# Scales shared out for several token blocks by one product, at other slots, and a larger ring of pieces for two weights

## The chip, the cores and the metric

One Trainium2 chip, one core of it. The metric is device time in microseconds of one execution, reference inputs, median over the runs shown. TensorE is PE in the profile, VectorE DVE, ScalarE ACT, GpSimd POOL, and SyncE (which issues the transfers) SP.

## The reference

Strided and local attention over 4 sequences of 576 tokens with 8 heads of 64, and behind it two feed-forward layers on the 2304 tokens of width 512. The first has 2048 hidden columns and the second 1536:

```python
h = x @ w_in
x = (h * np.cos(h)) @ w_out
g = x @ w_gate
y = (g * (1.0 / (1.0 + np.exp(-g))) * (x @ w_val)) @ w_out
```

The weights come as 8-byte words. The kernel multiplies in 16-bit floats: every operand is scaled by a power of two, split into a high and a low part, and three matmuls (high by high, high by low, low by high) stand for one product. For each split the kernel needs the largest magnitude of the whole operand on all 128 partitions.

## The kernel before, in words

The tokens lie in five blocks, three of 512 and two of 384 (`BLOCKS`), numbered 0 to 4. After attention comes **layer one**: for each block 16 slots, one for each 128 hidden columns. A slot is an up-projection `up1` (12 matmuls into a PSUM bank), an activation chain on ACT, DVE and POOL (`up1_a` on ACT, `up1_b` on DVE L577, `up1_c` on ACT, `up1_d` on DVE L584, `up1_e` on ACT and POOL L589), and, some slots later, a contraction `down1` (12 matmuls into four accumulators). The number of slots between (`lag`) shrinks from 12 to 2, so some slots hold two contractions. **Layer two** then runs over the same blocks, in six slots each, with products of halves of gate and val weights that a slot loads in one transfer.

PE runs strictly in the order of the code. It has four PSUM banks from `bank()` for the up-projections. A bank is free again when the last reader, L584 of two slots on, is done.

A scale is found in four steps. DVE reduces each 128x512 piece of the operand to one column (`scale_pieces`, L521, for tokens; `scan_raw`, L174, for weights). `spread_tops` (L120 to L130) reduces these columns to one, makes it a power of two and multiplies a 128x128 identity by it. `common_scale` (L136) multiplies the result by a matrix of ones on PE, into a whole PSUM bank, and DVE reduces that bank (L137) and makes the scale from it (L112 to L114). These products stand in PE's order between the contraction of one slot and the up-projection of the next. Token scales are `sx` (input of layer one) and `sy` (input of layer two), one per block.

While PE does layer one, the other engines prepare the weights. Work for that stands in a queue `fill`, with a cost for each step, and `pump` takes as many steps per slot as a share of the slot's matmul time pays for (`SHARE`, `SHARE2`). Token scales and splits stand in a second queue, `urgent`, of which one step is taken per slot (`pump_urgent`). In `fill` come, in this order, the conversion of w_out, the scans of gate and val, their scales, the twelve halves of gate and val (`pairs_later`), the scans of w_out2, its scale, and its conversion (`seven_later`). A half of gate and val goes through ACT (`g0`, L224), DVE (`g2` L231 and `g3` L235), four sums on POOL (L918), ACT (L245) and DVE (L248), and is then stored to DRAM. Its pieces live in a ring of homes, `unit_free`; a home that was stored comes back when the store has landed. Homes below `UNIT` (16) serve the activations, homes 16 to 23 are this ring, eight in all.

Of the kernel before, what the change touches and what calls it, by code (L numbers as in the profile page):

```python
# [59 lines left out]
HOMES, LATE, UNIT = 24, 4, 16  # L60
# [19 lines left out]
def build(tc, qk_l, qk_s, v_l, v_s, w_in, w_out, w_gate, w_val, w_out2, mask_l, mask_s, eye32, eye16, out):  # L80
    nc = tc.nc
    wide = w_in.dtype != F32
    with ExitStack() as ctx:
# [23 lines left out]
        def brief(name):  # L107
            return small.tile([128, 1], F32, name=name, bufs=2)

        def finish_scale(p, bound):  # L110
            s, inv = col("s"), col("inv")
# [5 lines left out]
        def spread_tops(parts, words):  # L117

            m, p = brief("m"), brief("p")
            nc.vector.tensor_reduce(out=m, in_=parts, op=ALU.max, axis=AX.X)  # L120
            if words:
                a = brief("a")
# [6 lines left out]
            d = small.tile([128, 128], BF16, name="tops", bufs=2)  # L129
            nc.vector.tensor_scalar(out=d, in0=id16, scalar1=p, scalar2=None, op0=ALU.mult)  # L130
            return d

        def common_scale(d, bound):

            t, p = bank()[:, 0:128], brief("q")
            nc.tensor.matmul(out=t, lhsT=ones16, rhs=d, start=True, stop=True)  # L136
            nc.vector.tensor_reduce(out=p, in_=t, op=ALU.max, axis=AX.X)  # L137
            return finish_scale(p, bound)
# [9 lines left out]
        parts_w = {k: small.tile([128, a.shape[0] + 1], F32, name=f"pw_{k}") for k, a in MATS.items()}  # L148
# [51 lines left out]
        def conv_steps(mat, j, dst, scan, free=load_raw):  # L200
# [38 lines left out]
            return box, [(0, g0)] + [(0.63, g1)] * scan + [(0.36, g2), (0.63, g3)]  # L239
# [45 lines left out]
        def top_later(mat):  # L285
            begin([])
            later(0.6, lambda: tops.__setitem__(mat, spread_tops(parts_w[mat], wide)))

        def scale_later(mat, bound):
            later(0.6, lambda: scale_w.__setitem__(mat, common_scale(tops[mat], bound)))  # L290
# [3 lines left out]
        def direct_later(mat, j, tiles):  # L294
# [4 lines left out]
            if j == 0:  # L299
                steps.append((0.6, lambda: scale_w.__setitem__(mat, common_scale(tops[mat], TW_OUT))))  # L300
# [214 lines left out]
        def scale_pieces(blk, scales):  # L515
            parts = small.tile([128, KC + 1], F32, name=f"parts{count[0]}_{blk}")
            count[0] += 1
            box = {}
            nc.gpsimd.memset(parts[:, KC:], TINY)
            for k in range(KC):  # L520
                yield 0.65, lambda k=k: nc.vector.tensor_reduce(out=parts[:, k:k + 1], in_=xy[blk][:, k, :], op=ALU.max, axis=AX.X,  # L521
                                                                apply_absolute_value=True)
            yield 0.6, lambda: box.__setitem__("top", spread_tops(parts, False))
            yield 0.6, lambda: scales.__setitem__(blk, common_scale(box["top"], TX))
# [234 lines left out]
        for j in range(M1):  # L759
            chain_later("in", j, wi)  # L760
            for cost, fn in list(scale_pieces(0, sx)) if j == XSAT else list(split_pieces(0, sx, xs)) if j == XSAT + 1 else ():
# [3 lines left out]
        scale_later("in", TW_IN)  # L765
# [95 lines left out]
        unit_free = deque(range(UNIT, HOMES))  # L861
# [76 lines left out]
        def open_weights(lag):  # L938

            if lag + 4 <= UNIT:  # L940
                most[0] = UNIT
            if not opened and most[0] == UNIT and max(taken, default=0) < UNIT:
                opened.append(True)
                scale_later("gate", TW_IN)
                scale_later("val", TW_IN)
# [5 lines left out]
            if len(opened) == 1 and lag < LATE and max(taken, default=0) < LATE:  # L951
# [4 lines left out]
                scale_later("out2", TW_LAST)  # L956
# [35 lines left out]
        def down_next():  # L992
# [18 lines left out]
        for blk in range(NBLK):  # L1011
            for m in range(M1):
# [11 lines left out]
                if m == (2 if blk else XM) and blk + 1 < NBLK:  # L1024
                    urge(scale_pieces(blk + 1, sx))
# [295 lines left out]
```

## Time and profile before

| | |
|---|---|
| median of 3 runs | 900.95 us (889.18 to 901.86) |
| profiled execution | 890.52 us, of which the span is 888.7 us |
| busy, of the span | PE 856.2 us (96%), DVE 657.0 (74%), ACT 521.9 (59%), POOL 197.9 (22%) |
| granted clock, mean | 0.987 |
| chain that ended last | PE 54%, DVE 3%, ACT 1%, POOL 1% |

A share of busy time is a mean over stages. Attention fills the first 110 us, layer one runs to about 506 us, layer two from there. A matmul counts as busy while it streams, so what matters on PE is the idle time before an instruction, what ended it, and the granted clock.

### The profile page before, as it was taken

To read this page: it belongs to the slowest core of one execution; us is meant where nothing else is said; L and a number is where in the kernel's file an instruction comes from. 1 tells how busy PE (TensorE), PEld (TensorE's weight loads), DVE (VectorE), ACT (ScalarE), POOL (GpSimd) and SP (SyncE) were. 2 spreads that over 40 slices of the span, in tenths; PEclk is the share of its full clock that TensorE was granted. 3 is DMA by queue.
4 is the path that set the end of the run, shared out by engine and by line. 5 is a ranking of instruction groups with operands and counts; after the bars stand their busy time and mean duration, and the time that the engine had idled before them with its cause. 6 is when DMAs were issued, how large, how long until landed. Compare 5 with 4: busy or idle time off the path is not lost.

```text
span 888.7 us, 18462 instructions
## 1 busy us (share of the span) xinstructions
PE 856.2 (96%) x7228; PEld 606.1 (68%) x7228; DVE 657.0 (74%) x1287; ACT 521.9 (59%) x1046; POOL 197.9 (22%) x253
## 2 busy tenths in 40 slices
PE   7999999999999989889999998999999999999998
PEld 4766644444444434445656687888888899999998
DVE  4987889994859977986999578757766665665562
ACT  4888988853446667555788566544544434544440
POOL 3443324221236545522222200000000000000000
PEclk7999999999999989999999999999999999999999
DMA  9998842576626555563445745666777678888894
GB/s 302 363 311 247 259 154 72 181 220 239 237 87 218 192 178 176 156 216 128 134 163 201 267 167 215 231 232 235 262 242 261 232 247 286 309 301 306 314 331 155
DMA packets 53512, 200.61 MB, mean 226 GB/s; under 512 B 5456, under 2 KB 16208, under 8 KB 49584
## 3 DMA queue, kind: packets, MB, share of 16 engines
q1 hardware_dynamic: 53424, 199.42, 65.9%
q8 instruction: 57, 0.93, 0.4%
q14 instruction: 31, 0.25, 0.1%
HBM read 175.41 MB, written 23.99 MB: 224 GB/s over the span
## 4 chain that ended last, share of the span: by engine, by line
PE 54%; DVE 3%; issue 1%; ACT 1%; POOL 1%; ACTq 0%; POOLq 0%; DVEq 0%
PE acc L694 14%; PE bank L541 10%; PE bank L543 10%; PE bank L542 10%; PE acc L541 4%; PE acc L543 4%; PE acc L542 4%; DVE arena L667 1%; DVE arena L1189 0%; POOL arena L918 0%; DVE arena L248 0%; DVE xs L248 0%; DVE wi L611 0%; ACT arena L664 0%; ACT arena L245 0%
## 5 line engine op out<-in xcount | busy, mean ns | idle before, releaser
L541 PE MATMUL bank<-xs,wi 128*128 128x256 f16 (+3 forms) x780 | 234.1, 300 | 16.5 <-DVE q L137 10.1
L543 PE MATMUL bank<-xs,wi 128*128 128x256 f16 (+3 forms) x780 | 234.3, 300 | 0.0
L542 PE MATMUL bank<-xs,wi 128*128 128x256 f16 (+3 forms) x780 | 234.2, 300 | 0.0
L589 POOL TENSOR_TENSOR arena<-tb,arena 128x512 f16<-128x512 f32 (+1 forms) x80 | 91.5, 1144 | 250.9 <-ACT arena L588 235.6
L542 PEld LDWEIGHTS <-wi 128*128 128x128 f16 x880 | 86.3, 98 | 55.8 <-issue 23.0
L541 PE MATMUL acc<-arena 128*128 128x512 f16 (+1 forms) x320 | 115.0, 359 | 0.0
L542 PE MATMUL acc<-arena 128*128 128x512 f16 (+1 forms) x320 | 114.7, 358 | 0.0
L543 PE MATMUL acc<-arena 128*128 128x512 f16 (+1 forms) x320 | 114.5, 358 | 0.0
L541 PEld LDWEIGHTS <-wi 128*128 128x128 f16 x880 | 86.3, 98 | 36.1 <-issue 1.7
L543 PEld LDWEIGHTS <-wi 128*128 128x128 f16 x880 | 86.4, 98 | 35.8 <-issue 1.6
L694 PEld LDWEIGHTS <-arena 128*128 128x128 f16 x1080 | 100.7, 98 | 8.2
L679 POOL TENSOR_TENSOR wi<-tb 128x256 f32<-128x256 f32 (+1 forms) x30 | 20.2, 674 | 340.6 <-DVE tb L661 340.6
L661 DVE SCALAR_TENSOR_TENSOR tb<-tb,c,arena 128x512 f32<-128x512 f32 (+1 forms) x60 | 41.6, 693 | 62.9 <-ACT tb L656 62.7
L574 ACT ACTIVATE tb<-bank,quarter,c 128x512 int32<-128x512 f32 (+1 forms) x75 | 54.4, 725 | 48.8 <-PE bank L543 37.1
L542 PEld LDWEIGHTS <-arena 128*128 128x128 f16 x600 | 58.8, 98 | 34.4 <-issue 1.9
L694 PE MATMUL acc<-arena 128*128 128x256 f16 (+1 forms) x702 | 82.0, 265 | 0.0
L543 PEld LDWEIGHTS <-arena 128*128 128x128 f16 x600 | 58.8, 98 | 33.1 <-issue 0.5
L541 PEld LDWEIGHTS <-arena 128*128 128x128 f16 x600 | 58.8, 98 | 33.0 <-issue 0.7
L664 ACT ACTIVATE arena<-tb 128x256 f16<-128x256 f32 (+3 forms) x59 | 28.9, 489 | 79.6 <-DVE tb L661 79.6
L1189 DVE TENSOR_TENSOR arena<-bank,cv 128x512 f32<-128x512 f32 (+1 forms) x60 | 38.1, 635 | 44.9 <-PE bank L543 44.3
L588 ACT ACTIVATE arena<-tb 128x512 f16<-128x512 f32 (+1 forms) x80 | 46.6, 582 | 38.3 <-PE acc L543 36.5
L541 PE MATMUL bank<-xs,arena 128*128 128x256 f16 (+1 forms) x240 | 62.9, 262 | 1.2 <-DVE arena L1189 1.2
(147 smaller groups left out, 1713.4 us busy)
## 6 DMA issues: line engine op xcount, KB each, us to landing
wi<-w SPq DMA_DIRECT2D x20, 1792.0 KB
arena<-w SPq DMA_DIRECT2D x60, 576.0 KB, 5.3
raw<-w_out SPq DMA_DIRECT2D x56, 512.0 KB, 4.5
arena<-w SPq DMA_DIRECT2D x10, 1792.0 KB
raw<-w_gate SPq DMA_DIRECT2D x24, 512.0 KB, 4.5
raw<-w_val SPq DMA_DIRECT2D x24, 512.0 KB, 4.8
w<-arena SPq DMA_DIRECT2D x42, 256.0 KB, 3.2
raw<-w_in SPq DMA_DIRECT2D x16, 512.0 KB
```

Source lines behind the costliest of these rows:

```text
L541: nc.tensor.matmul(out=o, lhsT=w[:, 0, c], rhs=x[0], start=first, stop=False, **kw)
L542: nc.tensor.matmul(out=o, lhsT=w[:, 0, c], rhs=x[1], start=False, stop=False, **kw)
L543: nc.tensor.matmul(out=o, lhsT=w[:, 1, c], rhs=x[0], start=False, stop=last, **kw)
L574: nc.scalar.activation(out=c["w"].bitcast(I32), in_=c["ph"], func=AF.Identity, scale=turn[c["blk"]], bias=quarter)
L588: nc.scalar.activation(out=g[:, 0, 0:n], in_=w, func=AF.Copy)
L589: nc.gpsimd.tensor_tensor(out=g[:, 1, 0:n], in0=w, in1=g[:, 0, 0:n], op=ALU.subtract)
L661: nc.vector.scalar_tensor_tensor(out=t, in0=t, scalar=s_g[c["blk"]], in1=c["C"][m][:, 1, 0:c["n"]], op0=ALU.mult, op1=ALU.mult)
L664: nc.scalar.activation(out=to, in_=src, func=AF.Copy, scale=2.0 ** -11)
L667: nc.vector.scalar_tensor_tensor(out=to, in0=hi, scalar=-2048.0, in1=src, op0=ALU.mult, op1=ALU.add)
L679: nc.gpsimd.tensor_tensor(out=t_sums[:, 0, 0:h], in0=c["t"][0][:, h:2 * h], in1=c["t"][0][:, 0:h], op=ALU.subtract)
L694: nc.tensor.matmul(out=o[:, c], lhsT=w[:, 256 * i + 128 * c:256 * i + 128 * c + 128], rhs=unit(u)[:, x:x + h], start=j == c == i == 0, sto ...
L1189: nc.vector.tensor_tensor(out=c["C"][m][:, :, h * right:h * right + h], in0=p, in1=t, op=ALU.add)
```

## The change

- `spread_tops`, `common_scale` and `finish_scale` take `n` operands: n columns, n scaled identities side by side, one product of 128n columns, one reduction to n columns.
- The scales of blocks 2, 3 and 4 for layer one are made together in block 1 (two scans to a slot). Before, block b+1's was made in block b.
- Layer two's scale of block 0 is made from slot 8 of block 3 on; those of blocks 1, 2 and 3 together from slot 4 of block 4 on (`MINLAG + 2`). Before, each followed the last contraction of its block. Block 4's stays in layer two.
- Gate's and val's scales are made by one product, after the scans of both.
- `FREE` = 12 takes the place of `UNIT` = 16 for the ring: homes 12 to 23, twelve in all. The ring opens when the activations need at most 12 homes.
- Costs that pace `fill`: gate's and val's scans 1.3 instead of 1.7; `g2` and `g3` of their conversion 0.5 and 0.8 instead of 0.36 and 0.63.

```diff
-HOMES, LATE, UNIT = 24, 4, 16
+HOMES, LATE, UNIT, FREE = 24, 4, 16, 12
...
-            d = small.tile([128, 128], BF16, name="tops", bufs=2)
-            nc.vector.tensor_scalar(out=d, in0=id16, scalar1=p, scalar2=None, op0=ALU.mult)
+            d = small.tile([128, 128 if n == 1 else 384], BF16, name="tops" if n == 1 else "tops3", bufs=2 if n == 1 else 1)
+            d = d[:, 0:128 * n].rearrange("p (n c) -> p n c", n=n)
+            for i in range(n):
+                nc.vector.tensor_scalar(out=d[:, i], in0=id16, scalar1=p[:, i:i + 1], scalar2=None, op0=ALU.mult)
             return d
 
-        def common_scale(d, bound):
-
-            t, p = bank()[:, 0:128], brief("q")
+        def common_scale(d, bound, n=1):
+
+            t, p = bank()[:, 0:128 * n].rearrange("p (n c) -> p n c", n=n), brief("q", n)
             nc.tensor.matmul(out=t, lhsT=ones16, rhs=d, start=True, stop=True)
             nc.vector.tensor_reduce(out=p, in_=t, op=ALU.max, axis=AX.X)
...
-            return box, [(0, g0)] + [(0.63, g1)] * scan + [(0.36, g2), (0.63, g3)]
+            return box, [(0, g0)] + [(0.63, g1)] * scan + ([(0.5, g2), (0.8, g3)] if mat in ('gate', 'val') else [(0.36, g2), (0.63, g3)])
...
-        unit_free = deque(range(UNIT, HOMES))
+        unit_free = deque(range(FREE, HOMES))
...
-            if lag + 4 <= UNIT:
-                most[0] = UNIT
-            if not opened and most[0] == UNIT and max(taken, default=0) < UNIT:
+            if lag + 4 <= FREE:
+                most[0] = FREE
+            if not opened and most[0] == FREE and max(taken, default=0) < FREE:
                 opened.append(True)
-                scale_later("gate", TW_IN)
-                scale_later("val", TW_IN)
+                scale_later(TW_IN, "gate", "val")
...
-                scan_later(mat, j, 1.7)
-            top_later(mat)
+                scan_later(mat, j, 1.3)
+        top_later("gate", "val")
...
             if m == M1 - 1:
-                if blk < NBLK - 1:
-                    urge(scale_pieces(blk, sy))
-                else:
-                    late_scale.extend(scale_pieces(blk, sy))
+                if blk == NBLK - 1:
+                    late_scale.extend(scale_pieces([blk], sy))
...
                 if m == (2 if blk else XM) and blk + 1 < NBLK:
-                    urge(scale_pieces(blk + 1, sx))
+                    if blk == 0:
+                        urge(scale_pieces([1], sx))
+                    elif blk == 1:
+                        urge(scale_pieces([2, 3, 4], sx, 2))
                     urge(split_pieces(blk + 1, sx, xs), ("xs", blk + 1))
+                if blk == NBLK - 2 and m == M1 // 2:
+                    urge(scale_pieces([0], sy))
+                if blk == NBLK - 1 and m == MINLAG + 2:
+                    urge(scale_pieces([1, 2, 3], sy, 2))
```

What becomes of the order of instructions is seen at three places. Line numbers of the change are its own: there L142 is the product, L143 its reduction, L559 to L561 the matmuls, L595 and L602 the steps `up1_b` and `up1_d`, L240, L244 and L257 the conversion and split of weights.

**Gate's and val's scales, on DVE.** Before (the step `up1_d`, L584, stands ahead of both reductions):

```order
L577 SCALAR_TENSOR_TENSOR tb<-bank,c_2528,tb 128x512
L521 TENSOR_REDUCE parts_0_3090<-xy_66 128x1
L120 TENSOR_REDUCE m<-pw_val 128x1
L130 TENSOR_SCALAR tops<-id_76,p 128x128
L584 SCALAR_TENSOR_TENSOR tb<-tb,bank 128x512
L137 TENSOR_REDUCE q<-bank 128x1
L137 TENSOR_REDUCE q<-bank 128x1
L231 TENSOR_SCALAR arena<-arena 128x512
```

The change:

```order
L595 SCALAR_TENSOR_TENSOR tb<-bank,c_2527,tb 128x512
L136 TENSOR_SCALAR tops_3264<-id_76,p_3259 128x128 x2
L143 TENSOR_REDUCE q_3268<-bank 128x2
L240 TENSOR_SCALAR arena<-arena 128x512
L244 SCALAR_TENSOR_TENSOR arena<-raw,arena 128x512
L602 SCALAR_TENSOR_TENSOR tb<-tb,bank 128x512
L240 TENSOR_SCALAR arena<-arena 128x512
L244 SCALAR_TENSOR_TENSOR arena<-raw,arena 128x512
L257 SCALAR_TENSOR_TENSOR arena<-arena,s_3271 128x512
L240 TENSOR_SCALAR arena<-arena 128x512
L244 SCALAR_TENSOR_TENSOR arena<-raw,arena 128x512
```

One reduction stands where two stood, one slot earlier in the program, and it and the first conversion now stand ahead of `up1_d`; seven more steps of conversion and split follow in the same slot.

**A layer-one scale in the middle of the conversion of gate and val, on PE** (block 3's, `sx`; the same slot in both). Before:

```order
L543 MATMUL acc_3758<-arena 128x512
L136 LDWEIGHTS ones_77
L136 MATMUL bank<-tops,ones_77 128x128
L541 LDWEIGHTS wi
L541 MATMUL bank<-xs,wi 128x512
```

The change:

```order
L561 MATMUL acc_3754<-arena 128x512
L559 LDWEIGHTS wi
L559 MATMUL bank<-xs,wi 128x512
```

The product is gone from there, and so are the other token products between gate's and val's scales and the end of their twelve halves (layer two's of blocks 0 and 1).

**The end of layer one, on DVE.** The change makes three `sy` scales there, in the last eight slots of block 4:

```order
L595 SCALAR_TENSOR_TENSOR tb<-bank,c_4917,tb 128x384
L537 TENSOR_REDUCE parts_5076<-xy_69 128x1 x2
L602 SCALAR_TENSOR_TENSOR tb<-tb,bank 128x384
L595 SCALAR_TENSOR_TENSOR tb<-bank,c_4917,tb 128x384
L124 TENSOR_REDUCE m_5494<-parts_5076 128x3
L132 TENSOR_SCALAR p_5495<-m_5494 128x3
L136 TENSOR_SCALAR tops_5498<-id_76,p_5495 128x128 x3
L602 SCALAR_TENSOR_TENSOR tb<-tb,bank 128x384
L595 SCALAR_TENSOR_TENSOR tb<-bank,c_4917,tb 128x384
L143 TENSOR_REDUCE q_5535<-bank 128x3
```

Before, these slots carried the last of w_out2's conversion, which in the change ends some five slots earlier.

## Rows read from the trace of the kernel before

**Rows 1.** The page: busy time, share of the span, instructions.

```profile
PE 856.2 (96%) x7228; PEld 606.1 (68%) x7228; DVE 657.0 (74%) x1287; ACT 521.9 (59%) x1046; POOL 197.9 (22%) x253
```

**Rows 2.** Stretches: length, busy PE PEld DVE ACT POOL (count), clock, DMA share, GB/s.

```profile
250.00:300.00 50.00, 49.59 (x229) 22.39 (x229) 42.57 (x72) 31.58 (x53) 28.38 (x29) 1.00 0.53 174
300.00:356.00 56.00, 51.46 (x225) 22.64 (x225) 46.72 (x75) 37.93 (x62) 30.92 (x31) 0.94 0.55 183
356.00:386.00 30.00, 24.66 (x121) 12.01 (x118) 24.67 (x42) 17.01 (x30) 13.20 (x16) 0.94 0.53 167
386.00:506.00 120.00, 117.86 (x727) 71.02 (x726) 101.98 (x200) 86.51 (x147) 30.51 (x33) 1.00 0.52 183
506.00:560.00 54.00, 48.60 (x435) 42.21 (x433) 39.73 (x70) 31.03 (x50) 3.64 (x5) 1.00 0.54 202
```

**Rows 3.** PE's waits, 200 to 500 us: total us, times, longest.

```profile
PE bank L541 <- DVE q L137: 10.1, 8, 4.1
PE bank L541 <- DVE tb L584: 2.8, 4, 1.6
PE bank L136 <- DVE tb L584: 0.3, 1, 0.3
```

**Rows 4.** PE in order of time: start, duration, instruction, [idle before it, releaser].

```profile
204.77 0.22 PE L136 MATMUL bank<-tops,ones 128*128 128x128 bf16 x1
205.37 0.38 PE L541 MATMUL bank<-xs,wi 128*128 128x512 f16 x1 [0.38 <-DVE q L137]
205.59 0.38 PE L542 MATMUL bank<-xs,wi 128*128 128x512 f16 x1
...
313.59 0.22 PE L136 MATMUL bank<-tops,ones 128*128 128x128 bf16 x1 [0.26 <-DVE tb L584]
317.87 0.58 PE L541 MATMUL bank<-xs,wi 128*128 128x512 f16 x1 [4.06 <-DVE q L137]
...
381.29 0.32 PE L541 MATMUL bank<-xs,wi 128*128 128x384 f16 x1 [2.78 <-DVE q L137]
...
452.70 0.32 PE L541 MATMUL bank<-xs,wi 128*128 128x384 f16 x1 [1.38 <-DVE q L137]
```

**Rows 5.** Two short stretches with a low clock, columns as in rows 2.

```profile
316.50:324.00 7.50, 6.13 (x16) 2.16 (x16) 5.45 (x13) 3.82 (x6) 2.81 (x4) 0.54 0.54 193
381.30:385.30 4.00, 4.00 (x14) 1.85 (x14) 2.45 (x7) 0.39 (x1) 0.75 (x2) 0.57 0.58 167
```

**Rows 6.** DVE in order of time around two products.

```profile
249.65 0.29 DVE L137 TENSOR_REDUCE q<-bank 128x1 f32<-128x128 f32 x1 [6.58 <-PE bank L136]
...
312.86 0.68 DVE L584 SCALAR_TENSOR_TENSOR tb<-tb,bank 128x512 f32<-128x512 f32 x1
...
317.54 0.28 DVE L137 TENSOR_REDUCE q<-bank 128x1 f32<-128x128 f32 x1
```

**Rows 7.** DVE by line and shape, 250 to 360 us (last: attention): busy, mean ns.

```profile
L248 DVE SCALAR_TENSOR_TENSOR arena<-arena,s 128x512 f16<-128x512 f32 x29 | 24.1, 837 | 5.0 <-ACT arena L245 5.0
L235 DVE SCALAR_TENSOR_TENSOR arena<-raw,arena 128x512 int32<-128x512 int32 x21 | 17.7, 841 | 0.3
L231 DVE TENSOR_SCALAR arena<-arena 128x512 int32<-128x512 int32 x22 | 14.9, 677 | 9.8 <-ACT arena L224 9.8
L521 DVE TENSOR_REDUCE parts<-xy 128x1 f32<-128x512 f32 x4 | 2.7, 672 | 0.0
L521 DVE TENSOR_REDUCE parts<-xy 128x1 f32<-128x384 f32 x4 | 2.2, 539 | 0.0
...
L443 DVE TENSOR_REDUCE mx<-bank 128x3 f32<-128x288 f32 x21 | 9.5, 451 | 8.0 <-PE bank L438 7.8
```

**Rows 8.** Waits of ACT (first row) and DVE, 250 to 380 us.

```profile
ACT arena L224 <- DMA w<-arena: 15.6, 13, 4.6
...
DVE arena L231 <- ACT arena L224: 10.6, 10, 2.9
DVE arena L248 <- ACT arena L245: 6.6, 4, 2.8
```

More of the change, by code (lines that the diff above doesn't have):

```diff
@@ L105, in col, with brief, cols, finish_scale @@
             return small.tile([128, 1], F32, name=f"{name}{count[0]}")
[L107 to L111, printed above, removed]
+        def brief(name, n=1):
+            return small.tile([128, n], F32, name=f"{name}{n}", bufs=2)
+        def cols(name, n):
+            count[0] += 1
+            return small.tile([128, n], F32, name=f"{name}{count[0]}")
+        def finish_scale(p, bound, n=1):
+            s, inv = cols("s", n), cols("inv", n)
             nc.vector.reciprocal(out=s, in_=p)
@@ L147, in build @@
         MATS = {"in": w_in, "out": w_out, "gate": w_gate, "val": w_val, "out2": w_out2}
-        parts_w = {k: small.tile([128, a.shape[0] + 1], F32, name=f"pw_{k}") for k, a in MATS.items()}
+        parts_w = {k: small.tile([128, a.shape[0] + 1], F32, name=f"pw_{k}") for k, a in MATS.items() if k not in ("gate", "val")}
+        parts_two = small.tile([128, 2, M2 + 1], F32, name="pw_two")
+        parts_w.update((k, parts_two[:, i]) for i, k in enumerate(("gate", "val")))
         for k, a in MATS.items():
@@ L299, in direct_later @@
             if j == 0:
-                steps.append((0.6, lambda: scale_w.__setitem__(mat, common_scale(tops[mat], TW_OUT))))
+                steps.append((0.6, lambda: set_scales(TW_OUT, mat)))
             steps.append((0, lambda: hi_part(tiles[j][:, 0], box["c"], scale_w[mat][0])))
@@ L513, in build, with scale_pieces, piece @@
         sx, xs, sy, ys = {}, {}, {}, {}
-        def scale_pieces(blk, scales):
-            parts = small.tile([128, KC + 1], F32, name=f"parts{count[0]}_{blk}")
-            count[0] += 1
+        def scale_pieces(blks, scales, at_once=1):
+            n = len(blks)
+            parts = cols("parts", n * (KC + 1)).rearrange("p (n k) -> p n k", n=n)
             box = {}
[L519 to L524, printed above, removed]
+            nc.gpsimd.memset(parts[:, :, KC:], TINY)
+            todo = [(i, k) for i in range(n) for k in range(KC)]
+            def piece(some):
+                for i, k in some:
+                    nc.vector.tensor_reduce(out=parts[:, i, k:k + 1], in_=xy[blks[i]][:, k, :], op=ALU.max, axis=AX.X,
+                                            apply_absolute_value=True)
+            for i in range(0, len(todo), at_once):
+                yield 0.65 * at_once, lambda some=todo[i:i + at_once]: piece(some)
+            yield 0.6, lambda: box.__setitem__("top", spread_tops(parts if n > 1 else parts[:, 0], False, n))
+            yield 0.6, lambda: scales.update(zip(blks, common_scale(box["top"], TX, n)))
         def split_pieces(blk, scales, dst):
@@ L760, in build @@
             chain_later("in", j, wi)
-            for cost, fn in list(scale_pieces(0, sx)) if j == XSAT else list(split_pieces(0, sx, xs)) if j == XSAT + 1 else ():
+            for cost, fn in list(scale_pieces([0], sx)) if j == XSAT else list(split_pieces(0, sx, xs)) if j == XSAT + 1 else ():
                 later(cost, fn)
```

24 lines of the change are left out of this document (14 added, 10 removed).

## The prediction

> **What bounds the kernel now.** I read the page first, then PE's waits by releaser, then PE in order of time around each wait, and last DVE, ACT and the granted clock around the longest ones. PE is busy for 856 of 888.7 us [rows 1], so there are 32 us to gain on PE without removing a matmul, and the question is which of them the edit touches. Between 200 and 500 us PE waits 13.2 us in all: 10.1 us in eight waits for L137, the reduction behind a spreading product, and 3.1 us for `up1_d` [rows 3]. In the rest of its idle time the edit changes nothing but layer two's first slots.
>
> The order of time shows how a product costs PE anything. The product takes 0.22 us. The next up-projection takes the bank that the product used, so it starts when DVE has reduced it: 0.38 us of idle time where DVE stood ready, as at 205.37 [rows 4]. Where DVE was behind, PE waited for all that stood ahead of L137 in DVE's order: 4.06 us at 317.87, 2.78 at 381.29, 1.38 at 452.70 [rows 4]. At 313.59 the product was already issued while DVE had just ended `up1_d`, and it came to L137 only at 317.54 [rows 6]. Both long waits lie in the conversion of gate and val, and behind both the granted clock is low: 0.54 over 7.5 us, 0.57 over 4 us [rows 5]. The levels are 1.2 and 2.4 GHz, so a mean of 0.54 is the low one for 0.92 of the stretch. Ahead of each drop PE had been idle for some 4 and 3 us; behind a wait of 1.6 us [rows 3] the clock between 356 and 386 fell only in that second place [rows 2, 5].
>
> DVE is why L137 came late. From 250 to 386 us it is busy for 114 of 136 us (42.6 + 46.7 + 24.7) [rows 2], and of its 22 idle us 17.2 are waits for ACT [rows 8], which itself waits 15.6 us in thirteen places for stores to free a home of the ring [rows 8].
>
> **The sum, against the profiled execution (890.5 us).**
>
> *Products that go.* The eight waits are 10.1 us [rows 3]: 8.2 in the three long ones, and five of about 0.38 [rows 4]. All these products leave their place: minus 10.1.
>
> *Products that stand instead.* Four are followed by an up-projection: three blocks together (384 columns), gate with val (256), w_out2 and layer two's block 0 (128 each). More columns cost twice. A matmul of 512 columns takes 0.22 us from start to start [rows 4], so 256 more are 0.11. DVE reduces 128 columns in 0.28 us [rows 6] and 288 in 0.451 [rows 7], some 1.05 ns a column, so 256 more are 0.27. That makes 0.38 + 0.38 = 0.76 for three blocks, 0.38 + 0.05 + 0.13 = 0.57 for the pair, and 0.38 each for the other two: plus 2.1. The lower bound is 0 (the next up-projection finds another bank), the upper one a late DVE for one of them, as at 381.29: plus 2.4 more, with 1.7 for the clock. I take 2.1, because the first two stand where DVE waits for PE (6.58 us ahead of L137 at 249.65 [rows 6]) and the others where it is busy for 102 of 120 us [rows 2]. The three-block product at the end of layer one is followed by contractions, which need no bank: nothing.
>
> *Clock.* Low for 0.92 x 7.5 = 6.9 us and 0.86 x 4 = 3.4 us [rows 5]. In the first, PE was idle for up to 1.4 us anyway (7.5 - 6.13). Half of the rest is lost: about 2.9 + 1.7 = 4.6 (4.4 to 5.1). Without the long waits it comes back: minus 4.6.
>
> *Waits for `up1_d`.* Now 3.1 us [rows 3]. Three things move. (a) Eleven token scans leave the stretch, seven of 512 and four of 384 columns: 7 x 0.672 + 4 x 0.539 = 6.9 us [rows 7]; what is left on DVE is about 107 us. (b) The twelve halves themselves (24 L231, 24 L235, 36 L248 of 512: 16 + 20 + 30 us [rows 7]) now fall on 19 slots instead of 21, because scans no longer use up their credit: two slots of matmuls less to hide under, some 10 of the 121 us that PE works at full clock there (125.7 [rows 2] less 4.6), and two `up1_b` and `up1_d` less on DVE, so about 104 against 111. (c) Twelve homes should take most of ACT's wait for stores, and with it DVE's 10.6 [rows 8]. With a third of the 17.2 left DVE needs 110 of 111 us. It starts late: the joint reduction waits for PE with a conversion behind it, so the slot's seven further steps, some 5 us, run into the next one. The four banks let DVE run late by a slot or so, about 5 us. I therefore leave 3.0 us of such waits in, as now. Bounds: 0, and 3 + two thirds of 17.2 less the spare us = 13, if the larger ring frees nothing.
>
> *Costed at nothing.* Layer two's scans of blocks 0 and 1 come into 386 to 506 us, eight of 0.672, and block 4's four of 0.539 leave: plus 3.2 of 18 idle us of DVE [rows 2]; if that cover were gone, w_out2's conversion, which now ends some five slots sooner, would give the time back. Block 2's split comes later in block 1, but its 13 urgent steps, one a slot from slot 2 on, end at slot 14 of 16. Scans of three blocks add 5 us to DVE in block 1; behind them it waited 6.58 us for PE [rows 6]. Layer two's first slots lose a product and its scans. PE idles 5.4 us there (54 - 48.6 [rows 2]); a gain of 0 to that is possible, and I take 0, since the sums and splits of block 1's tokens, which fill those slots, stay where they are. On SP one load of layer two's weights passes behind one store, and POOL loses two small memsets: nothing.
>
> Sum: -10.1 + 2.1 - 4.6 - 3.1 + 3.0 = -12.7, and 890.5 - 12.7 = **878 us**. The profiled execution lies 10.4 us below the median of the three runs, two of which are near 901 and one at 889; the trace shows nothing of the slower two. Against 900.95, 878 is 2.5% less, against 890.5 it is 1.4%. Within 2% a measurement can't tell it from no change.
>
> **Rivals.**
>
> *The runs' extra 10.4 us stays in the median* (0.27). The trace that I have is of the faster kind. If what makes other runs 901 lies outside 200 to 500 us, the change leaves it: 878 + 10.4 = 888. For it: attention, where transfers and clock could vary, is the same in both. Against it: the waits that go are those behind which the clock fell, so other runs may have lost more there. On this the Trainium skill, "TensorE: Matmul & The Clock Gate", section "What's actually happening", says that the gate's monitor runs free of the kernel's start, so that the same gap can cost differently from run to run; no run here shows it. By that rule the extra could be lost clock behind these waits, and then 878 would hold for every run.
>
> *The lateness was DVE's, not the products'* (0.17). Then the change does not do what it says: L137 only made visible that DVE was behind, and the next up-projections wait for `up1_d` instead. For it: 19 slots instead of 21, and a late start. Against it: 6.9 us of scans gone, and homes. If the two long waits (6.8 us) come back as bank waits, 885; with their 4.6 us of clock, 889.
>
> *Slower than the profiled run: the joint reduction holds DVE* (0.06). In the new order it stands ahead of `up1_d`, the conversion behind it. DVE idles 6.6 us there [rows 6] and the seven steps start after that. If also all 17.2 us of waits for ACT stay [rows 8], DVE needs 104 + 17.2 + 5 = 126 against 111 us, less a slot of slack of 5: 10; with the idle 6.6 not made up, 17, in waits long enough to lose 4.6 us of clock: 878 - 3 + 17 + 4.6 = 897. It decides from 15.6 us of such loss on, since that is what the products give (10.1 + 4.6 + 3.1 - 2.1).
>
> **Numbers.** Forecast 0.45 (874 to 883), extra in the median 0.27 (884 to 892), DVE late 0.17 (884 to 890), slower 0.06 (891 to 905), and 0.05 for more than forecast, below 874, if all small waits and some of layer two's go. The range of 871 to 891 leaves out the slower case and the tails. Faster by over 2%, below 883: the forecast less its upper edge, and the 0.05: 0.47. Slower by over 2%, above 919, needs a second such loss: 0.03. Within: 0.50. The likeliest case alone spans 874 to 883.
>
> **What would show it.** Waits for the reduction of about 2 us in all after 200 us, none above 1; a granted clock of 1.00 from 200 to 500 us; waits for `up1_d` of some 3 us, none above 2; ACT's wait for stores well under 15.6; the gap behind the three-block product near 0.76 us and behind the pair's near 0.57. Wrong would be: a wait of 3 us or more on PE in the conversion of gate and val, whatever it waits for; a clock below 1.00 there; or gaps as forecast and a time that is still near 890, which would put the loss into attention or layer two.

## The result, and the profile after

The changed kernel takes **881.33 us** (median of 4 runs, 880.38 to 883.31). The kernel before, run beside it, takes 898.42 us (889.18 to 901.86). Of undisturbed runs the ratio is **0.9887, with a 95% interval of 0.9838 to 0.9935**: 1.1% faster, against a level of before of 881.33 / 0.9887 = 891.4 us and not against its median here; the first experiment shows why these differ. The forecast of 878 was a gain of 2.5% on the median shown. The time lies in the range of 871 to 891, but the gain is 1.1% and not 2.5%: within the 2% that the prediction named, though its interval lies below 1.

The profiled execution took 880.38 us, 10.1 less than the one of before; 0.7 of this is attention (below). The page, and PE's waits from 200 to 500 us (total us, times, longest), for [rows 1] and [rows 3]; L143, L559 and L602 are the former L137, L541 and L584:

```profile
PE 851.0 (97%) x7223; PEld 604.9 (69%) x7223; DVE 658.8 (75%) x1256; ACT 522.0 (59%) x1046; POOL 202.5 (23%) x249
```

```profile
PE bank L559 <- DVE tb L602: 7.0, 8, 1.7
PE bank L559 <- DVE q L143: 1.5, 3, 0.6
PE acc L559 <- DVE xy L573: 0.7, 1, 0.7
```

The waits for the reduction fell from 10.1 to 1.5 us, and those for `up1_d` rose from 3.1 (2.8 and the product's own 0.3) to 7.0. The stretches that answer to [rows 2], shifted by the time gained (length, then busy time of PE, PEld, DVE, ACT, POOL, and the clock):

```profile
244.00:300.00 56.00, 53.65 (x249) 24.15 (x248) 49.81 (x70) 37.01 (x61) 30.33 (x30) 1.00 0.59 188
300.00:350.00 50.00, 47.74 (x220) 21.37 (x219) 46.95 (x65) 35.59 (x60) 34.54 (x32) 1.00 0.60 209
350.00:386.00 36.00, 33.41 (x181) 17.53 (x180) 31.38 (x56) 20.41 (x36) 11.98 (x12) 1.00 0.67 251
386.00:496.00 110.00, 109.30 (x677) 66.08 (x676) 91.86 (x175) 79.36 (x134) 31.02 (x32) 1.00 0.43 155
496.00:550.00 54.00, 48.59 (x434) 42.20 (x433) 38.18 (x62) 31.14 (x51) 3.64 (x5) 1.00 0.49 181
```

The granted clock is 1.00 in all five, where it was 0.94 in two. DVE is busy for 128 of the first 142 us, so it is still nearly full. Layer two's first slots (the last row) idle 5.4 us on PE, as before.

PE in order of time, for [rows 4]: the four new products' gaps, and between them the longest wait in the conversion of gate and val.

```profile
217.04 0.33 PE L142 MATMUL bank<-tops,ones 128*128 128x384 bf16 x1
218.01 0.38 PE L559 MATMUL bank<-xs,wi 128*128 128x512 f16 x1 [0.65 <-DVE q L143]
...
244.70 0.38 PE L559 MATMUL bank<-xs,wi 128*128 128x512 f16 x1 [0.52 <-DVE q L143]
...
282.59 0.38 PE L559 MATMUL bank<-xs,wi 128*128 128x512 f16 x1 [1.48 <-DVE tb L602]
...
380.99 0.22 PE L142 MATMUL bank<-tops,ones 128*128 128x128 bf16 x1
382.88 0.32 PE L559 MATMUL bank<-xs,wi 128*128 128x384 f16 x1 [1.67 <-DVE tb L602]
...
414.68 0.32 PE L559 MATMUL bank<-xs,wi 128*128 128x384 f16 x1 [0.38 <-DVE q L143]
```

Three blocks cost 0.65, the pair 0.52, layer two's block 0 0.38. The wait of 1.67 follows w_out2's product at 380.99, but it stands under L602 in the table. DVE's order shows why:

```profile
381.75 0.61 DVE L257 SCALAR_TENSOR_TENSOR xs<-xy,s,xs 128x384 f16<-128x384 f32 x1
382.28 0.55 DVE L602 SCALAR_TENSOR_TENSOR tb<-tb,bank 128x384 f32<-128x384 f32 x1
382.75 0.28 DVE L143 TENSOR_REDUCE q<-bank 128x1 f32<-128x128 f32 x1
```

DVE was late, and came to the reduction 1.5 us after the product had ended. PE did not wait for that reduction: it started at 382.88, behind the end of `up1_d` at 382.83 and ahead of the end of L143 at 383.03. So it took another bank than the product's, one that `up1_d` frees. I charge the 1.67 to the product, because the product had taken one of the four banks; that PE would have found one free without it is argued, not shown.

**Where the time came from.** Attention varies from run to run, so I measure from the first matmul behind its end to the end of the span; all that the sum speaks of lies in there. (It belongs to layer one's second slot; the first slot runs some 9 us earlier, inside attention.) That matmul starts here in the kernel before:

```profile
113.67 0.38 PE L541 MATMUL acc<-xs,wi 128*128 128x512 f16 x1 [0.63 <-ACT xy L501]
```

and in the changed one here:

```profile
113.00 0.38 PE L559 MATMUL acc<-xs,wi 128*128 128x512 f16 x1 [0.63 <-ACT xy L514]
```

The rest is then 888.7 - 113.67 = 775.0 us before and 878.6 - 113.00 = 765.6 after: **-9.4 us**. By the terms of the sum: products that went -10.1, new ones +3.2 (0.65 + 0.52 + 1.67 + 0.38), `up1_d` from 3.1 to 5.3 (7.0 less the 1.67): +2.2. That leaves 4.7 for the clock, where the prediction had estimated 4.6; the traces show directly only that it no longer fell. This "rest" is what the experiments below are compared by. It is read from one trace of each kernel; where a kernel was traced twice, the two agree within 0.4 us.

### The profile page after: what moved, and what is told of

Read it like the earlier page. It is cut to its first block, busy times and chain, and to the rows that moved or that the text cites. A ratio compares the mean times of both kernels' runs of the same rounds, so it can differ in the third digit from the quotient of the medians.

```text
span 878.6 us, 18390 instructions
## 1 busy us (share of the span) xinstructions
PE 851.0 (97%) x7223; PEld 604.9 (69%) x7223; DVE 658.8 (75%) x1256; ACT 522.0 (59%) x1046; POOL 202.5 (23%) x249
## 4 chain that ended last, share of the span: by engine, by line
PE 74%; issue 6%; POOL 6%; DVE 5%; DMA 4%; ACT 4%; SPq 0%; POOLq 0%; ACTq 0%; DVEq 0%
PE acc L712 14%; PE bank L559 12%; PE bank L561 11%; PE bank L560 11%; PE acc L559 6%; PE acc L561 6%; PE acc L560 6%; POOL arena L936 3%; PE bank L448 2%; POOL arena L607 2%; PE po L501 2%; DMA vl<-v_l 1%; DMA v_pair<-v_s 1%; DVE arena L257 1%; ACT tb L592 1%
## 5 line engine op out<-in xcount | busy, mean ns | idle before, releaser
L559 PE MATMUL bank<-xs,wi 128*128 128x256 f16 (+3 forms) x780 | 232.6, 298 | 12.2 <-DVE tb L602 7.2
L561 PE MATMUL bank<-xs,wi 128*128 128x256 f16 (+3 forms) x780 | 232.6, 298 | 0.0
L607 POOL TENSOR_TENSOR arena<-tb,arena 128x512 f16<-128x512 f32 (+1 forms) x80 | 94.1, 1176 | 234.0 <-ACT arena L606 213.8
L559 PE MATMUL acc<-arena 128*128 128x512 f16 (+1 forms) x320 | 114.5, 358 | 0.0
L561 PE MATMUL acc<-arena 128*128 128x512 f16 (+1 forms) x320 | 114.5, 358 | 0.0
L559 PEld LDWEIGHTS <-wi 128*128 128x128 f16 x880 | 86.1, 98 | 35.1
L561 PEld LDWEIGHTS <-wi 128*128 128x128 f16 x880 | 86.1, 98 | 34.8
L561 PEld LDWEIGHTS <-arena 128*128 128x128 f16 x600 | 58.7, 98 | 32.8
L559 PEld LDWEIGHTS <-arena 128*128 128x128 f16 x600 | 58.7, 98 | 32.6
L559 PE MATMUL bank<-xs,arena 128*128 128x256 f16 (+1 forms) x240 | 62.9, 262 | 1.2 <-DVE arena L1211 1.2
```

The costliest lines, as they stand in the source:

```text
L559: nc.tensor.matmul(out=o, lhsT=w[:, 0, c], rhs=x[0], start=first, stop=False, **kw)
L561: nc.tensor.matmul(out=o, lhsT=w[:, 1, c], rhs=x[0], start=False, stop=last, **kw)
L607: nc.gpsimd.tensor_tensor(out=g[:, 1, 0:n], in0=w, in1=g[:, 0, 0:n], op=ALU.subtract)
```

## The experiments

The changed kernel differs from the one before in three things that can be set apart: the joint products, the ring of twelve homes instead of eight (the constant `FREE`, 24 - 12), and the costs by which the planner spaces scans (1.3 instead of 1.7) and conversions (0.5 and 0.8 instead of 0.36 and 0.63).

### The kernel before, again

No edit.

> The kernel before, unchanged, in five more rounds, for the spread of its runs. If the spread (889 to 902 us) is lost TensorE clock behind the long waits, the runs' span must fall with their mean granted clock: 12 us more is 24 us more at the low level, so a run of 901 should show a mean clock near 0.96 where 889 shows 0.987. If it comes from the transfers of the attention stage, runs near 901 and near 889 show the same mean clock within 0.005.

891.72 us (12 runs, 888.2 to 898.25) beside 891.1 (29 runs, 886.58 to 900.26); ratio 0.9997 [0.9964, 1.003]. The runs of both with a mean clock of 0.984 or more took 886.6 to 892.3, those with 0.975 or less 896.2 to 900.3. The profiled one is of the second kind, 896.17. PE's waits from 200 to 500 us are what they were, so this run's extra does not lie behind the long waits, as the first theory had it:

```profile
PE bank L541 <- DVE q L137: 10.1, 8, 4.1
PE bank L541 <- DVE tb L584: 2.7, 4, 1.6
PE bank L136 <- DVE tb L584: 0.3, 1, 0.3
```

The clock was lower, as that theory also asked (0.975 against 0.987 over the span), but in attention. Here is its stretch from 12 to 50 us in the trace of before that the prediction was made from:

```profile
12.00:50.00 38.00, 35.15 (x522) 24.87 (x523) 31.06 (x84) 30.56 (x114) 16.52 (x26) 0.87 1.03 357
```

and here in this run:

```profile
12.00:50.00 38.00, 34.62 (x338) 23.65 (x340) 19.63 (x54) 21.26 (x72) 11.49 (x19) 0.55 0.91 310
```

```profile
119.70 0.38 PE L541 MATMUL acc<-xs,wi 128*128 128x512 f16 x1 [0.63 <-ACT xy L501]
```

In these 38 us PE issued 522 matmuls at a clock of 0.87, and 338 at 0.55. The low level lasted about 34 us ((1 - 0.55) x 2 x 38) against 10, and the rest began 6.0 us later; it is 774.7 us long, within 0.4 us of the first trace. The kernel's level is 891: medians of 891.1, 891.51 and 891.55 in three sets of 29, 13 and 11 runs. That the 900.95 was a slow draw of attention's clock follows from this, but no trace of that run was kept.

### The changed kernel, again

No edit.

> The changed kernel once more, in five rounds, for its spread. If what spreads the runs of the kernel before (886.6 to 900.3 us, falling with their mean clock) is the clock in attention, which is the same in both kernels, then the changed kernel spreads as far, 876 to 890 us, also falling with the mean clock, and its median lies 9 to 10 us below the median of before (near 882). If the spread came from the two long waits, its runs stay within 4 us of each other.

884.1 us (6 runs, 880.81 to 895.36) against 891.55 (11 runs); ratio 0.99 [0.9855, 0.9944]. Here too the run with the lowest clock (0.973) is the longest. In the profiled execution, 887.37, the rest began at 119.41 us and not 113.00; it is 765.9 us long, with waits of 7.3 for `up1_d` and 1.5 for reductions. The granted clock was low in two places of attention, 0.78 over 12 to 50 us and 0.74 over 70 to 90, where the first trace of the changed kernel has 0.82 and 1.00. So the spread is there with the change too, 881 to 895 us; the first four runs had little of it. The two theories had asked for 876 to 890, falling with the clock, or for 4 us; the first one holds, some 5 us higher, and the median lies 7.5 us below that of before, where 9 to 10 were expected.

### The products alone

Old costs and the ring of eight homes, joint products as changed:

```diff
-HOMES, LATE, UNIT, FREE = 24, 4, 16, 12
+HOMES, LATE, UNIT, FREE = 24, 4, 16, 16
-            ... + ([(0.5, g2), (0.8, g3)] if mat in ('gate', 'val') else [(0.36, g2), (0.63, g3)])
+            ... + [(0.36, g2), (0.63, g3)]
-                scan_later(mat, j, 1.3)
+                scan_later(mat, j, 1.7)
```

> Only the products are changed (joined, at other slots); ring of eight homes and costs of before. Theory 1: 880 to 884, no wait for a reduction above 1 us, clock 1.00 from 200 to 500 us. Theory 2: DVE as late as before (idle 17 us for ACT in the conversion), and PE's 6.8 us of long waits come back as waits for up1_d, with or without their clock: 885 to 890.

892.16 us (10 runs, 888.46 to 901.51), ratio 1.0001 [0.9962, 1.004]; the rest 774.1 us, 0.9 below the kernel before. The median lies above both theories' ranges, the profiled 888.46 within that of theory 2. PE's waits, 200 to 500 us, and the two longest, in order of time:

```profile
PE bank L559 <- DVE tb L602: 11.0, 7, 3.8
PE bank L559 <- DVE q L143: 1.9, 4, 0.6
```

```profile
315.46 0.38 PE L559 MATMUL bank<-xs,wi 128*128 128x512 f16 x1 [2.26 <-DVE tb L602]
...
370.84 0.32 PE L559 MATMUL bank<-xs,wi 128*128 128x384 f16 x1 [3.79 <-DVE tb L602]
```

The products' waits fell from 10.1 to 1.9, and 11.0 us for `up1_d` stand in their place: the 2.26 close to where the 4.06 of [rows 4] had stood, the 3.79 some 10 us ahead of the 2.78. The clock fell twice again, for some 3.4 us each. By themselves the products' new places were worth 0.9 us: the old ones had mostly made visible that DVE was behind, which is the second rival.

### The ring and the costs without the products

The kernel before, with `FREE = 12`, 1.3, 0.5 and 0.8:

```diff
-HOMES, LATE, UNIT = 24, 4, 16
+HOMES, LATE, UNIT, FREE = 24, 4, 16, 12
-            ... + [(0.36, g2), (0.63, g3)]
+            ... + ([(0.5, g2), (0.8, g3)] if mat in ('gate', 'val') else [(0.36, g2), (0.63, g3)])
-        unit_free = deque(range(UNIT, HOMES))
+        unit_free = deque(range(FREE, HOMES))
-            if lag + 4 <= UNIT:
+            if lag + 4 <= FREE:
...
-                scan_later(mat, j, 1.7)
+                scan_later(mat, j, 1.3)
```

> The kernel before with the ring of twelve homes and the new costs, the products where they were. Theory 1: at least one product in the conversion of gate and val still meets a late DVE: waits for reductions of 6 us or more, clock below 1.00 there, 886 to 891. Theory 2: DVE is in time, waits for reductions fall to about 3 us (eight of 0.38) and the clock stays at 1.00: 879 to 883.

887.77 us (10 runs, 884.79 to 895.66), ratio 0.9949 [0.9917, 0.9982]; the rest 771.6, 3.4 less than before.

```profile
PE bank L541 <- DVE q L137: 9.4, 6, 4.5
PE bank L136 <- DVE q L137: 0.8, 2, 0.4
PE bank L541 <- DVE tb L584: 0.8, 1, 0.8
```

The waits for `up1_d` nearly went, the ones behind products stayed, one of them 4.55 us at 326.90 and one 2.30 at 386.14, with two drops of the clock. That is the first theory. So neither half does it alone: the products alone give 0.9 us and leave the lateness at `up1_d`, the ring and the costs alone give 3.4 and leave it at the products, and both together give 9.4. Beside the ring and the costs the products are worth 6.0 us (771.6 - 765.6).

### The ring alone, at old and at new costs

All as changed but eight homes (`FREE = 16`):

```diff
-HOMES, LATE, UNIT, FREE = 24, 4, 16, 12
+HOMES, LATE, UNIT, FREE = 24, 4, 16, 16
```

> The changed kernel with the ring of pieces back at eight homes (it then opens at 16), costs and products as changed. Theory 1 (the products' places made the gain): no wait for a reduction above 1 us, clock 1.00 from 200 to 500 us, time within 2 us of the changed kernel (880 to 883). Theory 2 (the ring made it: DVE is no longer held by ACT's wait for stores): ACT waits 10 us or more for stores again, waits for up1_d rise from 5.3 by at least 5 us, time 886 to 890.

881.76 us (4 runs, 880.62 to 882.05), ratio 0.987 [0.9816, 0.9924]; the rest 765.5, that of the changed kernel. ACT's wait for the stores that free a home, the 15.6 us of [rows 8], is back in full:

```profile
ACT arena L233 <- DMA w<-arena: 15.6, 9, 3.6
```

In the changed kernel's trace ACT has no such wait over 244 to 380 us. DVE's waits for ACT are 12.7 us with eight homes (7.8 for L240, 4.9 for L257) and 8.1 with twelve (1.9 and 6.2), so the larger ring does give DVE time. But PE's waits are the same without it (6.7 and 1.5). At the new costs the ring costs PE nothing.

The other corner is twelve homes and the joint products at the old costs:

```diff
-            ... + ([(0.5, g2), (0.8, g3)] if mat in ('gate', 'val') else [(0.36, g2), (0.63, g3)])
+            ... + [(0.36, g2), (0.63, g3)]
-                scan_later(mat, j, 1.3)
+                scan_later(mat, j, 1.7)
```

> Products and ring as changed, both costs as before. With the changed costs the ring made no difference (765.5 from the end of attention with eight homes, 765.6 with twelve), and without costs and ring the products gave nothing (774.1). Theory F (at the old costs the steps stand so densely that the ring binds): 769 or less, no drop of the clock between 200 and 500 us. Theory G (the ring is idle in either case and the two costs together make the rest): 772 or more, waits for up1_d of 9 us or more.

885.51 us in one run; the rest 770.2, 4.0 less than with eight homes. PE waits 7.9 us for `up1_d`, its longest 3.80, and the clock falls twice. Neither theory's figures came: the rest lies between them. At the old costs the ring is worth 4 us, at the new ones nothing. In this order the 9.4 us are products 0.9, ring 4.0, costs 4.6; with the costs ahead of the ring they are products 0.9, costs 8.6 and the ring nought.

### The costs one by one

Scans at the old 1.7, so that gate's and val's maxima are spread out as before:

```diff
-                scan_later(mat, j, 1.3)
+                scan_later(mat, j, 1.7)
```

> The changed kernel with one cost put back: gate's and val's scans at 1.7 instead of 1.3. Read by the time from the end of attention to the end of the span, which the clock in attention doesn't touch (before 775.1, changed 765.6, products alone 774.1). Theory A (an earlier start of the conversion is what the costs bring, so that it ends among the 512-token slots): 771 or more. Theory B (fewer conversion steps in each slot are what they bring): 768 or less, waits for up1_d near 5 us.

883.37 us (4 runs, 877.49 to 884.3), ratio 0.9891 [0.983, 0.9952]; the rest is 762.1, 3.5 less than the changed kernel's, and PE waits 2.8 us for `up1_d`, where theory B had asked for 5. That an earlier start of the conversion was the gain (theory A) is refuted at these conversion costs: the old cost of the scans is better. The run times alone don't tell the two apart, 883.37 against 881.33 and 884.1.

The conversion's steps at the old 0.36 and 0.63:

```diff
-            ... + ([(0.5, g2), (0.8, g3)] if mat in ('gate', 'val') else [(0.36, g2), (0.63, g3)])
+            ... + [(0.36, g2), (0.63, g3)]
```

> The changed kernel with the other cost put back: 0.36 and 0.63 for the two conversion steps. From the end of attention: theory A 767 or less; theory B 771 or more, with waits for up1_d of 9 us or more and at least one drop of the clock between 250 and 400 us.

883.35 us (10 runs, 881.1 to 893.9), ratio 0.9918 [0.9879, 0.9956]; the rest 767.3, 1.7 more than the changed kernel's, and 7.6 us of waits in eleven pieces, none above 1.6, with the clock at 1.00. Theory B had asked for 771 or more and a drop of the clock: right in sign, too large, and the figure is nearly theory A's (767 or less). Beside the run with both old costs, 770.2 in the section above, it shows that the two costs don't add. At the old conversion costs the scans at 1.3 gain 2.9 us (770.2 to 767.3), at the new ones they lose 3.5 (762.1 to 765.6); the new conversion costs gain 1.7 us beside scans at 1.3 and 8.1 beside scans at 1.7. So what a cost is worth hangs on where the other one puts the steps.

The same costs moved the other way, so that fewer steps fall into a slot:

```diff
-            ... + ([(0.5, g2), (0.8, g3)] if mat in ('gate', 'val') else [(0.36, g2), (0.63, g3)])
+            ... + ([(0.65, g2), (1.05, g3)] if mat in ('gate', 'val') else [(0.36, g2), (0.63, g3)])
```

> The changed kernel with still higher costs, 0.65 and 1.05: about two slots more for the twelve halves. Theory B: waits for up1_d fall from 5.3 us to 3 or less, 762 to 764 from the end of attention. Theory C (what is left of these waits comes from DVE instructions that GpSimd's stretch, and from the chain through GpSimd, not from the number of steps in a slot): 5 us of waits stay, 765 to 767.

879.67 us (4 runs, 875.75 to 883.26), ratio 0.9863 [0.9799, 0.9926]; the rest 760.1, 5.5 less than the changed kernel's, below the 762 to 764 of theory B, and the lowest of all kernels that compute everything.

```profile
PE acc L559 <- DVE xy L573: 1.6, 1, 1.6
PE bank L559 <- DVE q L143: 1.5, 3, 0.6
PE bank L559 <- DVE tb L602: 1.5, 1, 1.5
```

Of the waits for `up1_d` one of 1.5 us is left. So the changed kernel's 5.3 us came from how many conversion steps the planner put into one slot, with GpSimd's sums in place. Wider spacing also keeps more of the steps apart from the sums: L240 takes 0.645 us on average there and L244 0.848, where they took 0.807 and 0.901. Theory C, by which 5 us would have stayed, is refuted.

### What makes DVE late: GpSimd's sums

The 44 sums of L936 in this stretch run on GpSimd, beside DVE's conversion. Here they write zeros and read nothing:

```diff
-                nc.gpsimd.tensor_tensor(out=out, in0=a, in1=b, op=op)
+                nc.gpsimd.memset(out, 0.0)
```

> The changed kernel with GpSimd's four sums of each half replaced by writes of zeros to the same places: GpSimd reads nothing there, and the products of layer two are not the reference's. If DVE's conversion and split are stretched because GpSimd reads and writes at the same time, their means between 244 and 350 us fall from 0.807, 0.901 and 0.906 us to near the 0.42, 0.68 and 0.74 that they take alone, waits for up1_d fall below 1.5 us and the time from the end of attention to 761 to 763. If only the order and the chain hold DVE, the durations stay above 0.65, 0.85 and 0.85.

881.65 us in one run, with a late attention; the rest 759.6, 6.0 less than the changed kernel's and below the expected 761 to 763. DVE by line and shape over 244 to 350 us (busy, mean ns), in the changed kernel:

```profile
L257 DVE SCALAR_TENSOR_TENSOR arena<-arena,s 128x512 f16<-128x512 f32 x31 | 27.9, 906 | 5.4 <-ACT arena L254 5.4
L244 DVE SCALAR_TENSOR_TENSOR arena<-raw,arena 128x512 int32<-128x512 int32 x22 | 19.8, 901 | 0.3
L240 DVE TENSOR_SCALAR arena<-arena 128x512 int32<-128x512 int32 x23 | 18.6, 807 | 1.9 <-ACT arena L233 1.9
L595 DVE SCALAR_TENSOR_TENSOR tb<-bank,c,tb 128x512 f32<-128x512 f32 x17 | 12.5, 738 | 0.0
L602 DVE SCALAR_TENSOR_TENSOR tb<-tb,bank 128x512 f32<-128x512 f32 x17 | 11.5, 674 | 0.0
```

and without the sums:

```profile
L257 DVE SCALAR_TENSOR_TENSOR arena<-arena,s 128x512 f16<-128x512 f32 x31 | 26.7, 867 | 10.4 <-ACT arena L254 10.4
L244 DVE SCALAR_TENSOR_TENSOR arena<-raw,arena 128x512 int32<-128x512 int32 x22 | 15.1, 687 | 0.3
L595 DVE SCALAR_TENSOR_TENSOR tb<-bank,c,tb 128x512 f32<-128x512 f32 x17 | 12.6, 742 | 0.0
L602 DVE SCALAR_TENSOR_TENSOR tb<-tb,bank 128x512 f32<-128x512 f32 x17 | 11.5, 678 | 0.0
L240 DVE TENSOR_SCALAR arena<-arena 128x512 int32<-128x512 int32 x23 | 10.5, 458 | 3.9 <-ACT arena L233 3.8
```

L244 falls from 901 to 687 ns and L240 from 807 to 458, while L595 and L602, which read one operand from a PSUM bank, stay. So the steps of the conversion are lengthened by what GpSimd does beside them: 4.7 + 8.1 + 1.2 = 14 us over this stretch. Of the waits for `up1_d` in the conversion none is left; the 2.0 us that PE still waits for L602 are 1.67 behind w_out2's product and 0.32 at 447 us.

L257 did not fall to the expected 0.74 us. One GpSimd instruction that reads was kept, the subtraction of `up1_e` (L607), and L257 meets it. Two places of this run, with DVE's and GpSimd's rows put together:

```profile
263.15 1.16 POOL L607 TENSOR_TENSOR arena<-tb,arena 128x512 f16<-128x512 f32 x1 [4.02 <-ACT arena L606]
263.65 1.20 DVE L257 SCALAR_TENSOR_TENSOR arena<-arena,s 128x512 f16<-128x512 f32 x1 [1.01 <-ACT arena L254]
...
268.83 0.74 DVE L257 SCALAR_TENSOR_TENSOR arena<-arena,s 128x512 f16<-128x512 f32 x1
269.20 1.39 POOL L607 TENSOR_TENSOR arena<-tb,arena 128x512 f16<-128x512 f32 x1 [3.61 <-ACT arena L606]
```

The one that begins second is lengthened: L257 takes 1.20 us behind L607 and 0.74 ahead of it, L607 1.39 behind L257 and 1.16 ahead of it. In the changed kernel, the place before the 1.48 us wait of PE at 282.59 shows the sums' part one by one, on DVE:

```profile
277.75 1.32 DVE L257 SCALAR_TENSOR_TENSOR arena<-arena,s 128x512 f16<-128x512 f32 x1 [3.02 <-ACT arena L254]
279.00 0.94 DVE L240 TENSOR_SCALAR arena<-arena 128x512 int32<-128x512 int32 x1
279.98 1.10 DVE L244 SCALAR_TENSOR_TENSOR arena<-raw,arena 128x512 int32<-128x512 int32 x1
281.03 0.92 DVE L240 TENSOR_SCALAR arena<-arena 128x512 int32<-128x512 int32 x1
281.87 0.67 DVE L602 SCALAR_TENSOR_TENSOR tb<-tb,bank 128x512 f32<-128x512 f32 x1
```

and on GpSimd:

```profile
277.80 3.86 POOL L936 TENSOR_TENSOR arena<-arena 128x256 f32<-128x256 f32 x4
```

While the four sums run, every step beside them is long, and `up1_d` stands behind. The experiment also frees ACT of its waits for the sums (10.1 us before, 0.6 here), so its 6 us are not DVE's durations alone; that the durations fall is read directly.

### Holding the joint reduction back, and a better pace

An empty step of cost 2.0 ahead of the pair's product, so that fewer conversion steps share its slot:

```diff
                 opened.append(True)
+                later(2.0, lambda: None)
                 scale_later(TW_IN, "gate", "val")
```

> The changed kernel with an empty step of cost 2.0 ahead of gate's and val's product, so that its reduction and the first conversion stand behind up1_d in DVE's order and fewer steps follow in that slot. If the joint reduction holds DVE (the third rival of the prediction), waits for up1_d fall from 5.3 us by 2 or more and the time from the end of attention from 765.6 to 763.5 or less. If not, it stays within 1 us.

879.54 us in one run; the rest 763.8, 1.9 less than the changed kernel's. The waits early in the conversion went; one of 3.03 us is there at 361.53, with one drop of the clock. Without the 1.20 behind w_out2's product the waits for `up1_d` are 3.3 us, 2.0 less, as expected; the rest misses the expected 763.5 by 0.3. That the joint reduction's hold was what cost this is not shown, because the empty step also moves all the steps behind it. Against it: in the changed kernel the first wait for `up1_d` comes some 37 us after that reduction, and DVE stood idle for 3.02 us just ahead of it (277.75 above), so it was not behind any more. Both remedies together, the empty step and costs of 0.6 and 0.95:

```diff
-            ... + ([(0.5, g2), (0.8, g3)] if mat in ('gate', 'val') else [(0.36, g2), (0.63, g3)])
+            ... + ([(0.6, g2), (0.95, g3)] if mat in ('gate', 'val') else [(0.36, g2), (0.63, g3)])
+                later(2.0, lambda: None)
```

> Candidate: the changed kernel with conversion costs 0.6 and 0.95 and the empty step of 2.0. Waits for up1_d 2 us or less, 760 to 762 from the end of attention (765.6 changed, 760.1 with costs 0.65 and 1.05 alone), median 4 to 5 us below the changed kernel's in the same rounds.

878.65 us (6 runs, 877.02 to 890.29), ratio to the kernel before 0.9855 [0.9804, 0.9905]; the rest 763.1. In the same rounds the changed kernel stood at 884.1 and 0.99 [0.9855, 0.9944]: the intervals overlap, and by the rest the two are 2.8 us apart. PE waits 3.6 us for `up1_d`, where 2 or less was expected, and the rest misses the expected 760 to 762. By the same measure the costs of 0.65 and 1.05 alone, 760.1, are the better version.

## Why the prediction was right or wrong

**The comparison failed first.** The sum started from the profiled 890.5 and gave -1.4%; -1.1% was measured. The forecast of -2.5% came from setting 878 against 900.95, the median of three runs, with the words that the trace shows nothing of the slower two. So the 10.4 us between them were taken as gained, with no row for it. What the runs showed in its place: the kernel's level is 891, its runs get longer as their mean clock falls, and the slow one that was traced lost its time in attention. The first rival had it right in kind: the extra lies in attention, and the edit leaves it. Its number, 888, did not follow, because the extra falls on runs of both kernels by chance; it is not a constant to be added. The prediction weighed lost clock behind the waits that go. The repeated run of before has the same waits and the same rest within 0.4 us, so there the two runs lost the same; all its extra is in attention. The rule of the Trainium skill that was weighed with it ("TensorE: Matmul & The Clock Gate", "What's actually happening"), that the gate's monitor runs free of the kernel's start, may bear on attention; no run here shows whether it does.

**The products' waits** (-10.1) went as forecast, and the drops of the clock with them; the granted clock is 1.00 over 200 to 500 us, and the other terms leave 4.7 us for it (forecast 4.6).

**The new products** (+2.1) cost 3.2. Three blocks 0.65 (forecast 0.76), the pair 0.52 (0.57), layer two's 0.38 (0.38). Behind w_out2's product PE waited 1.67 where 0.38 stood, for a bank that `up1_d` frees; the upper bound had allowed for one late DVE, and this was it, without a loss of clock.

**The waits for `up1_d`** (3.0 left in) came to 5.3, and this is the term of the sum that was mis-sized most. The prediction priced DVE's conversion steps at the means of [rows 7]: 0.677, 0.841 and 0.837. After the change they took 0.807, 0.901 and 0.906; on the 76 steps of 512 columns that is 3.0 + 1.3 + 2.1 = 6.4 us more of DVE. More of them ran beside a GpSimd instruction: 52 of those 76, where it was 41 of the 72 of [rows 7]. That these 6.4 us made the extra 2.3 us of waits is argued, not shown; without the sums the waits go, but with wider spacing and the sums in place they nearly go too. That ACT's wait for stores would go, and DVE would gain by it, came true (DVE's waits for ACT fell from 17.2 to 8.1 us, a third of 17.2 was forecast), but PE gained nothing by it: with eight homes its waits are the same.

**The reason was wrong where the size came out.** Waits for L137 were read as the products' price, and five of 0.38 us were. The two long ones, 6.8 us and their clock, were DVE's lateness, as the second rival had it: the products alone gave 0.9 us. But that rival is only half of it, since the ring and the costs alone gave 3.4 of the 9.4 us and left two long waits at the products. The prediction gave the products all the gain and the raised costs none; of the conversion's pace it counted only the net (19 slots instead of 21), as a loss. That the sum came near is in this part luck: the edit happened to hold both halves. Nearly all the signs that it had named came (waits for reductions 1.5 us, the clock at 1.00, no wait above 2, gaps of 0.65 and 0.52), and they could not tell the two halves apart.

**Costed at nothing:** layer two's first slots idle 5.4 us as before ([rows 2] and the last row of the stretches above); the three-block product at the end of layer one shows no wait over 200 to 500 us; block 1's extra scans lay where DVE waits for PE (6.3 us ahead of the pair's reduction, 6.58 before). These held. (In the third rival 10.1 + 4.6 + 3.1 - 2.1 is 15.7, not 15.6; nothing hangs on it.)

**Open:** why the clock in attention is low for 10 us in one run and 34 in another was not tried. Why scans at 1.3 gain at one pace of the conversion and lose at the other was not traced to single steps. Nor was it tried whether moving the sums to another engine gives back the 6 us that their absence gave.

## What to carry to other kernels

When a wait names a small instruction behind a late engine, ask what stood ahead of it in that engine's order: removing the small one may only move the wait to the next consumer. One run with that part alone and one with all but that part show it; here neither alone gave the gain. Price an engine's steps by what runs beside them after the change, not by their mean before it. And before a forecast is set against a median, find out what spreads the runs, and compare by a stretch that begins behind it.

## What the runs showed that was not expected

**GpSimd lengthens DVE's steps.** With the sums L240 took 807 ns on average and 458 without, L244 901 and 687; L595, with one operand in PSUM, 738 and 742. Counted one by one in the changed kernel, 244 to 350 us, the steps of 512 columns that no GpSimd instruction overlaps take 0.41 to 0.43 us (L240), 0.68 to 0.69 (L244) and 0.73 to 0.75 (L257); those that one overlaps take 0.92, 1.05 and 0.99 on average. The Trainium skill, "SBUF — State Buffer", section "Who interferes with whom", says that a DVE instruction with two SBUF inputs, or a `tensor_scalar` in its fast mode, contends with a GpSimd instruction that reads SBUF, and that the one that comes second is blocked until the other is done. The trace agrees on which instructions suffer and which don't, and that it is the second to begin (L257 1.20 us behind L607 and 0.74 ahead of it, above). Whether it stood blocked or ran slower the records don't tell: beside four sums of 0.97 us each (3.86 / 4) L257 took 1.32 us.

**Attention's clock spreads the runs.** Those of the kernel before reach from 886.6 to 900.3 us and follow the mean clock; in the two that were profiled the rest of the program is the same within 0.4 us.
